# Windowed attention and two MoE layers on one core: attention masks added in PSUM by products with the identity for four groups, weight splits on ACT and VectorE

## The chip, the core and the metric

The kernel runs on one core of a Trainium2 chip. Its engines are TensorE (PE: matmul and transposes; PEld is its weight load), VectorE (DVE), ScalarE (ACT), GpSimd (POOL) and SyncE (SP), which issues the DMAs; each works through a queue of its own in order, and waits on semaphores of the others. SBUF holds the tiles, PSUM the results of TensorE. The metric is the device time of the program in microseconds (us); lower is better.

## What is computed

Inputs are q, k and v (2 batches, 8 heads, 768 positions, 64 dimensions, float32) and the weights of two feed-forward layers in float64. Attention sees a window of 16 positions on either side, and besides it one row for each block of 32 positions: the maximum of k and the mean of v.

```python
k_sum = k.reshape(B, H, nb, 32, D).max(axis=3)
v_sum = v.reshape(B, H, nb, 32, D).mean(axis=3)
scores_l = where(abs(i - j) < 16, scale * q @ k.T, -1e9)
scores_s = scale * q @ k_sum.T + log(32)
a = softmax(concatenate([scores_l, scores_s], -1))
x = a @ concatenate([v, v_sum])             # 1536 tokens x 512
x = (relu(x @ w_in) ** 2) @ w_out           # 512 x 2048, 2048 x 512
xn = x / rms(x) * rms_g
out = (silu(xn @ w_gate) * (xn @ w_val)) @ w_out2   # 512 x 1536, twice, and 1536 x 512
```

## The kernel before

**Tiles.** The 1536 tokens are 12 groups of 128, six to a batch. A group's scores fill two PSUM tiles `s0`, `s1` of 128 x 480: four heads each, with 120 columns a head (24 block rows and a window of 96 positions). Every product of the feed-forward layers is made of three (`mm3`, `ff_out`): both factors are split into a high part (fp32r) and a low part (the rest), as `xhi`/`xlo`, `hhi`/`hlo` and `w_`.

**A group.** `scores` makes 16 products into `s0` and `s1`. `softmax` has VectorE add the mask and write the sum to the SBUF tile `t` (L444), take the maximum of each head (L448), and ACT the exponential with its sum, head by head (L450); VectorE divides. Groups 0 to 2 do this in two parts of four heads, later ones in one. `ptrans` transposes `t` into `pps`, which ACT copies to `pT` (L471). `av` multiplies with `vx`, the rows of v and the means, into `xps` (L491), which ACT and VectorE split into `xhi` and `xlo` (L481, L482). Since `vx` has four slots, `vload` of a later group (L407, on SP) waits for `xps` of an earlier one. `qprep` transposes q two groups at a time (L366, copy L367), `prep_k` k. `vmean` makes the means of v by products with a constant (L379).

**Weights.** They come as 64-bit words (`load64`: `raw_wi`, `raw_wo`, DMA on SP). `conv_a` lets ACT read the two words (L176, L177), `conv_b` lets VectorE put a float32 together in four instructions (L183 to L190), and `split` makes `w_`: for the first eight tiles (`wi0` to `wi3`, `wo0` to `wo3`) on GpSimd (cast L197, subtraction L200), for the later ones on ACT and VectorE. `Units.tick` moves this pipeline by one step.

**Stages.** A start phase prepares k, q and the first scores. Then the first round of the first layer runs in six pairs of groups, with the attention of the following groups woven in: `h_pair` makes h of two weight tiles (L512), `y_pair` adds them to `y` (L533), so that TensorE has products of the layer while ACT and VectorE do the softmax. After that only the layers' own products are left; there TensorE does nothing else until the end.

**What sets the order.** Each engine's order is made when the program is built, by the Tile scheduler: it goes by its own forecast of the time and by the program's order. PSUM tiles of the attention rotate over four tags with two slots each in the first groups, then over `a` and `x`; of the tags, `y` and `h` are those of the layers. A tile's slot is given on when its last reader is done.

Two definitions decide what runs where around the change:

```python
def EXPACT(g): return g % 4 != 1 or g == 1     # maxima negated, exps on ACT head by head
def PARTS(g): return 2 if g < 3 else 1         # softmax in two parts
```

Of the kernel before, what the change touches and what calls it, by code (L numbers as in the profile page):

```python
# [10 lines left out]
F32 = mybir.dt.float32  # L11
F32R = mybir.dt.float32r
U32 = mybir.dt.uint32
I32 = mybir.dt.int32
AF = mybir.ActivationFunctionType
ALU = mybir.AluOpType
AX = mybir.AxisListType
# [15 lines left out]
def tile_window_attention_moe_moe2(  # L33
# [43 lines left out]
    scale = 1.0 / math.sqrt(D)  # L77

    cpool = ctx.enter_context(tc.tile_pool(name="cpool", bufs=1))
    wpool = ctx.enter_context(tc.tile_pool(name="wpool", bufs=1))  # L80
    xpool = ctx.enter_context(tc.tile_pool(name="xpool", bufs=NCH))
    hpool = ctx.enter_context(tc.tile_pool(name="hpool", bufs=2))
# [5 lines left out]
    ident = cpool.tile([P, P], F32, name="ident")  # L88
    make_identity(nc, ident)
    um = cpool.tile([P, KW + QT], F32, name="um")  # L90
    masks = {}
    ind = cpool.tile([P, NB + P // (BLK // 2) * (NC2 - 1)], F32, name="ind")
    ss = cpool.tile([P, NG], F32, name="ss")
    rinv = cpool.tile([P, NG], F32, name="rinv")
# [1 line left out]
    def constants():  # L96
        n = ind.shape[1]
        o = P // (BLK // 2) * (NC2 - 1)
        pb = BLK // 2
        nc.gpsimd.memset(ind, 1.0 / BLK)  # L100
        nc.gpsimd.affine_select(
            out=ind, in_=ind, compare_op=ALU.is_ge, fill=0.0, base=pb * o,
            pattern=[[-pb, n]], channel_multiplier=1,
        )
        nc.gpsimd.affine_select(
            out=ind, in_=ind, compare_op=ALU.is_ge, fill=0.0, base=pb - 1 - pb * o,
            pattern=[[pb, n]], channel_multiplier=-1,
        )
        nc.gpsimd.memset(um, 0.0)
        nc.gpsimd.affine_select(  # L110
            out=um, in_=um, compare_op=ALU.is_ge, fill=NEG, base=-1,
            pattern=[[1, KW + QT]], channel_multiplier=-1,
        )
        nc.gpsimd.affine_select(
            out=um, in_=um, compare_op=ALU.is_ge, fill=NEG, base=2 * WIN - 1,
            pattern=[[-1, KW + QT]], channel_multiplier=1,
        )


        mid = cpool.tile([P, NK], F32, name="mask_mid")  # L120
        nc.gpsimd.memset(mid, math.log(BLK))
        for j, n, o in ((0, G0, 0), (K1, QT, G0)):
            nc.gpsimd.tensor_copy(mid[0:QT, j : j + n], um[0:QT, o : o + n])
            nc.gpsimd.tensor_copy(mid[QT:P, j : j + n], um[QT:P, QT + o : QT + o + n])
        first = cpool.tile([P, NK], F32, name="mask_first")
        nc.gpsimd.tensor_copy(first, mid)
        nc.gpsimd.memset(first[0:QT, 0:WIN], NEG)
        last = cpool.tile([P, NK], F32, name="mask_last")
        nc.gpsimd.tensor_copy(last, mid)
        nc.gpsimd.memset(last[QT:P, NK - WIN : NK], NEG)  # L130
        masks.update(first=first, mid=mid, last=last)

# [55 lines left out]
        nc.vector.tensor_tensor(xi, xi, r, op=ALU.add)  # L190
        return x

    def split(x, nm, pool):
        w_ = wslot(f"w_{nm}")
        hi, lo = w_[:, 0], w_[:, 1]
        if pool:
            nc.gpsimd.tensor_copy(hi, x)  # L197
        else:
            nc.scalar.copy(hi, x)
        (nc.gpsimd if pool else nc.vector).tensor_tensor(lo, x, hi.bitcast(F32), op=ALU.subtract)  # L200
        return hi, lo

    class Units:
# [9 lines left out]
        def tick(self):  # L213
            n, units = self.n, self.units
            if n[3] < n[2]:
                u = units[n[3]]
                W[u] = split(self.x.pop(u), "%s%d" % u, n[3] < 2 * ROUNDS1[0])
                n[3] += 1
            if n[2] < n[1]:
                u = units[n[2]]  # L220
                with after(*((("mx", 0),) if n[2] == 0 else ())):
                    self.x[u] = conv_b(*self.a.pop(u))
                n[2] += 1
            if n[1] < n[0]:
                u = units[n[1]]
                self.a[u] = conv_a(self.raw.pop(u), "%s%d" % u)
                n[1] += 1
            self.load(min(n[2] + self.ahead, len(units), self.used + self.cap))
# [182 lines left out]
    def scores(g):  # L411
        b, r = divmod(g, GPB)
        qT = state[("qT", g)][:, :, (r % 2) * P : (r % 2 + 1) * P]
        sl = [psA(f"s{e}_{g}", [P, NPAIR, NK]) for e in range(2)]
        for p in range(NPAIR):
            for x in range(2):
                for e in range(2):
# [4 lines left out]
                        sl[e][QT * u : QT * u + QT, p, :],  # L422
                        qT[rr, p, QT * u : QT * u + QT],
                        kT[rr, p, o : o + NK],
                        start=True, stop=True,
                    )
        state[("s", g)] = sl

    def softmax(g):
# [10 lines left out]
        for i in range(parts):  # L440
            hs = slice(n * i, n * i + n)
            tv, m_, s_ = t[:, hs], mx[:, hs], sm[:, hs]
            for e in range(2 // parts * i, 2 // parts * (i + 1)):
                nc.vector.tensor_tensor(  # L444
                    te[:, e], sl[e], mk.unsqueeze(1).to_broadcast([P, NPAIR, NK]), op=ALU.add
                )
            if EXPACT(g):
                mark[("mx", g)] = nc.vector.reduce_max(m_, tv, axis=AX.X, negate=True)  # L448
                for h in range(hs.start, hs.stop):
                    mark[("exp", g)] = nc.scalar.activation(  # L450
                        t[:, h], t[:, h], AF.Exp, bias=mx[:, h : h + 1], accum_out=sm[:, h : h + 1]
                    )
            else:
                nc.vector.reduce_max(m_, tv, axis=AX.X)
# [406 lines left out]
```

## Time and profile before

| | us |
|---|---|
| three runs | 667.84, 668.17, 668.64 |
| median | 668.17 |
| the profiled execution | 667.06 |
| its span (first to last instruction) | 665.4 |
| busy in it: TensorE | 642.0 (96%) |
| VectorE | 402.9 (61%) |
| ACT | 304.6 (46%) |
| GpSimd | 27.3 (4%) |

The profile is one execution. Its span lies 1.7 us below the time of that execution, which in turn lies 1.1 us below the median. TensorE is busy for nearly the whole span, and GpSimd only in its first 100 us; but a share over the span is a mean over stages, and the attention lies in the first 120 us or so. There a table by stretches, the timelines of the engines and the SP queue tell what TensorE waits for. [...]

### The profile page before, as it was taken

Reading aid. Unit: us, or ns where it says so; the run is one execution under the profiler, and the core shown is the slowest. Engines: PE = TensorE matmul, PEld = TensorE weight load, DVE = VectorE, ACT = ScalarE, POOL = GpSimd, SP = SyncE. Lnnn points to the kernel's source line nnn. Section 1 sums busy time; section 2 is a strip of 40 time slices with the busy share of each in tenths; the row PEclk is TensorE's granted clock in tenths of the full one; section 3 lists DMA queues with packets and bytes.
Section 4 is the critical chain, followed back from the end, with each engine's and each line's share of the span. In section 5 each row is a group of like instructions: output and inputs, shape, how many; then the busy total and the mean of one; then the engine's idle time right before and its main releaser. Section 6 shows DMA issues by size and latency. Waiting matters only on the chain.

```text
span 665.4 us, 9357 instructions
## 1 busy us (share of the span) xinstructions
PE 642.0 (96%) x3644; PEld 530.8 (80%) x3644; DVE 402.9 (61%) x716; ACT 304.6 (46%) x656; POOL 27.3 (4%) x45
## 2 busy tenths in 40 slices
PE   7768997999999999999999999999999999999997
PEld 6566976888888888888888888888888888888885
DVE  4798777759999389528484894299613271313132
ACT  4875666557675266227253773267411231111110
POOL 3153110000000000000000000000000000000000
PEclk9878998999999999999999999999999999999999
DMA  9994644215412313101131351025300000001011
GB/s 241 290 222 112 152 136 142 75 39 179 138 64 95 96 64 96 32 1 64 32 96 32 97 162 60 1 60 161 97 0 1 0 1 0 1 1 63 1 64 64
DMA packets 76957, 53.70 MB, mean 81 GB/s; under 512 B 45040, under 2 KB 71664, under 8 KB 76912
## 3 DMA queue, kind: packets, MB, share of 16 engines
q1 hardware_dynamic: 76912, 53.09, 27.0%
q8 instruction: 29, 0.48, 0.3%
q14 instruction: 16, 0.13, 0.1%
HBM read 49.94 MB, written 3.15 MB: 80 GB/s over the span
## 4 chain that ended last, share of the span: by engine, by line
PE 87%; DVE 5%; SPq 3%; ACT 2%; issue 1%; DMA 1%; DVEq 0%; ACTq 0%
PE y L533 19%; PE h L512 18%; PE v L512 15%; PE g L512 15%; PE z L533 15%; ACT t L450 2%; PE xps L491 2%; PE pps L470 1%; SPq L308 1%; PE s L421 1%; SPq L407 1%; PE vmean L379 1%; PE xps L503 1%; PE qps L366 1%; DMA qr<-in_q_dram 1%
## 5 line engine op out<-in xcount | busy, mean ns | idle before, releaser
L512 PE MATMUL h<-xhi,w_wi 128*128 128x512 f32 (+1 forms) x480 | 134.2, 352 | 1.3 <-ACT xhi L481 1.3
L533 PE MATMUL y<-w_wo,hhi 128*128 128x512 f32 x384 | 119.0, 394 | 0.1
L807 DVE TENSOR_TENSOR sg<-v,sg 128x512 f32<-128x512 f32 x36 | 24.9, 691 | 131.2 <-PE v L512 131.2
L512 PEld LDWEIGHTS h<-xhi,w_wi 128*128 128x128 f32 x480 | 86.3, 192 | 13.3 <-ACT xhi L481 1.5
L512 PE MATMUL v<-xhi,w_wv 128*128 128x512 f32 x288 | 94.8, 390 | 0.0
L512 PE MATMUL g<-xhi,w_wg 128*128 128x512 f32 x288 | 94.5, 390 | 0.0
L533 PE MATMUL z<-w_wp,hhiz 128*128 128x512 f32 x288 | 88.0, 389 | 0.0
L512 PE MATMUL h<-xlo,w_wi 128*128 128x512 f32 (+1 forms) x240 | 84.4, 352 | 3.0 <-DVE xlo L482 3.0
L533 PEld LDWEIGHTS y<-w_wo,hhi 128*128 128x128 f32 x384 | 71.5, 189 | 14.8 <-ACT hhi L523 0.4
L533 PE MATMUL y<-w_wo,hlo 128*128 128x512 f32 x192 | 74.2, 394 | 0.2 <-DVE hlo L524 0.2
L805 ACT ACTIVATE sg<-g 128x512 f32<-128x512 f32 x36 | 21.5, 597 | 102.1 <-PE g L512 99.9
L512 PEld LDWEIGHTS v<-xhi,w_wv 128*128 128x128 f32 x288 | 54.1, 188 | 11.2
L512 PEld LDWEIGHTS g<-xhi,w_wg 128*128 128x128 f32 x288 | 54.0, 188 | 11.2
L533 PEld LDWEIGHTS z<-w_wp,hhiz 128*128 128x128 f32 x288 | 54.0, 188 | 11.1
L660 ACT ACTIVATE r<-h 128x512 f32<-128x512 f32 x48 | 28.6, 596 | 67.5 <-PE h L512 67.4
L512 PE MATMUL v<-xlo,w_wv 128*128 128x512 f32 x144 | 56.1, 389 | 0.0
L512 PE MATMUL g<-xlo,w_wg 128*128 128x512 f32 x144 | 56.0, 389 | 0.0
L533 PE MATMUL z<-w_wp,hloz 128*128 128x512 f32 x144 | 55.4, 389 | 0.0
L523 ACT CAST hhiz<-sg 128x512 fp32r<-128x512 f32 x36 | 22.3, 620 | 68.6 <-DVE sg L807 68.3
L512 PEld LDWEIGHTS h<-xlo,w_wi 128*128 128x128 f32 x240 | 46.2, 192 | 8.8 <-DVE xlo L482 3.2
L661 DVE TENSOR_TENSOR r<-h,r 128x512 f32<-128x512 f32 x48 | 32.9, 685 | 32.4 <-ACT r L660 32.4
L533 PEld LDWEIGHTS y<-w_wo,hlo 128*128 128x128 f32 x192 | 36.0, 189 | 8.1 <-DVE hlo L524 0.6
(133 smaller groups left out, 918.7 us busy)
## 6 DMA issues: line engine op xcount, KB each, us to landing
raw_wi<-in_moe_w_in_dram SPq DMA_DIRECT2D x16, 512.0 KB, 4.9
raw_wo<-in_moe_w_out_dram SPq DMA_DIRECT2D x16, 512.0 KB, 4.3
raw_wg<-in_moe_w_gate_dram SPq DMA_DIRECT2D x12, 512.0 KB, 3.5
raw_wv<-in_moe_w_val_dram SPq DMA_DIRECT2D x12, 512.0 KB, 3.6
raw_wp<-in_moe_w_out_dram SPq DMA_DIRECT2D x12, 512.0 KB, 3.5
kr<-in_k_dram SPq DMA_DIRECT2D x12, 256.0 KB, 4.2
qr<-in_q_dram SPq DMA_DIRECT2D x12, 256.0 KB, 3.9
vr<-in_v_dram SPq DMA_DIRECT2D x6, 512.0 KB, 4.9
```

Of the source, the lines that this page charges most:

```text
L308: nc.sync.dma_start(t[:, j].rearrange("p (h d) -> p h d", h=H), src[b, :, o : o + P, :].rearrange("h p d -> p h d"),)
L366: nc.tensor.transpose(ps[:, p, :], qr[:, j, p * P : (p + 1) * P], ident)
L379: nc.tensor.matmul(ps, ind[:, nb2 * (NC2 - 1 - c) : nb2 * (NC2 - 1 - c) + NB], vr[:, :, e, :], start=(c == 0 and e == 0), stop=(c == NC2 - ...
L450: mark[("exp", g)] = nc.scalar.activation(t[:, h], t[:, h], AF.Exp, bias=mx[:, h : h + 1], accum_out=sm[:, h : h + 1])
L491: nc.tensor.matmul(ps[QT * e : QT * e + QT, o : o + QT], vx[:, (2 * g + u) % NVX, 2 * p + e, :], pT[:, e * NPAIR + p, QT * u : QT * u + QT ...
L512: nc.tensor.matmul(ps, a_, b_, start=(i == 0), stop=(i == tot - 1))
L523: nc.scalar.copy(hi[:, 0:n], s[:, 0:n])
L533: nc.tensor.matmul(y, a_[:, ms], b_, start=(first and i == 0), stop=(last and i == 2))
L660: nc.scalar.activation(t, ps, AF.Relu)
L661: nc.vector.tensor_tensor(t, ps, t, op=ALU.mult)
L805: nc.scalar.activation(t, psg, AF.Silu)
L807: nc.vector.tensor_tensor(t, psv, t, op=ALU.mult)
```

## The change

**Masks.** For groups 0 to 3 (`NPE`) the mask is no longer added by VectorE. A product of the identity (`identr`) with the mask's high part (`mhi`), repeated for the four heads of a tile, opens the accumulation in `s0` and `s1`; the 16 score products add to it; a product with the low part (`mlo`) closes it. The maxima and the exponentials then read PSUM and not `t`. Group 3, whose one maximum covered 960 columns, takes two of 480, one for each PSUM tile. GpSimd makes `identr`, two high parts and the low part (that of `mid`) at the start.

**Splits.** `split` has no GpSimd branch any more: the first eight weight tiles are cast by ACT and subtracted by VectorE, as the others were already.

**Tiles.** A constant tile of 24 columns (`left`) is put first in `cpool`, beside the new constants.

The scheduler makes a new order out of this. On ACT, around the copies of `pT5` (group 5's transposed weights), before:

```order
L367 ACTIVATE qT6_929<-qps6_0_930 128x4x128
L367 ACTIVATE qT6_929<-qps6_1_936 128x4x128
L660 ACTIVATE r0_1_2_1054<-h0_1_2_1029 128x512
L471 COPY pT5_974<-pps5_0_975 120x512
L523 CAST hhi0_1_2_1057<-r0_1_2_1054 128x512
L471 COPY pT5_974<-pps5_1_981 120x512
L176 ACTIVATE x_wi4_1696<-raw_wi4_1493 128x512
L177 ACTIVATE u_wi4_1697<-raw_wi4_1493 128x512
L481 CAST xhi1_1_925<-xps1_5_1061 128x4x128
L388 COPY vm1_1087<-vmean1_1080 24x512
```

and now:

```order
L508 CAST xhi1_1_943<-xps1_4_926 128x4x128
L376 ACTIVATE qT6_947<-qps6_0_948 128x4x128
L376 ACTIVATE qT6_947<-qps6_1_954 128x4x128
L498 COPY pT5_992<-pps5_0_993 120x512
L573 COPY yp3_1202<-y0_1_1_1149 128x512
L188 ACTIVATE x_wi4_1714<-raw_wi4_1511 128x512
L189 ACTIVATE u_wi4_1715<-raw_wi4_1511 128x512
L498 COPY pT5_992<-pps5_1_999 120x512
L508 CAST xhi1_1_943<-xps1_5_1079 128x4x128
L397 COPY vm1_1105<-vmean1_1098 24x512
```

The second copy of `pT5` stands behind the two reads of `raw_wi4` and no longer ahead of them; the copy of y (`yp3`) stands ahead of both, and the copies of q's transposes ahead of `pT5`, as they did.

On TensorE, from the h products of the second pair to those behind xps of group 4, before:

```order
L512 MATMUL h0_1_2_1029<-xhi1_0_416,w_wi3_685 128x256
L512 MATMUL h0_1_2_1029<-xlo1_0_417,w_wi3_685 128x256
L331 MATMUL kps1_2_1_889<-ident_77,kr1_2_774 128x128 x4
L512 MATMUL h0_1_2_1029<-xhi1_0_416,w_wi3_685 128x256
L491 MATMUL xps1_4_908<-pT4_813,vx_90 64x64 x16
L366 MATMUL qps6_0_930<-ident_77,qr6_645 128x128 x4
L366 MATMUL qps6_1_936<-ident_77,qr6_645 128x128 x4
L512 MATMUL h0_1_2_1029<-xhi1_0_416,w_wi3_685 128x256
```

and now:

```order
L560 MATMUL y0_1_0_1148<-w_wo0_797,hhi0_1_0_988 128x512
L560 MATMUL y0_1_0_1148<-w_wo0_797,hlo0_1_0_989 128x512
L560 MATMUL y0_1_1_1149<-w_wo0_797,hhi0_1_0_988 128x512 x2
L560 MATMUL y0_1_1_1149<-w_wo0_797,hlo0_1_0_989 128x512
L560 MATMUL y0_1_0_1148<-w_wo1_814,hhi0_1_0_988 128x512 x2
L560 MATMUL y0_1_0_1148<-w_wo1_814,hlo0_1_0_989 128x512
L560 MATMUL y0_1_1_1149<-w_wo1_814,hhi0_1_0_988 128x512 x2
L560 MATMUL y0_1_1_1149<-w_wo1_814,hlo0_1_0_989 128x512
L518 MATMUL xps1_4_926<-pT4_831,vx_95 64x64 x16
L375 MATMUL qps6_0_948<-ident_78,qr6_663 128x128 x4
L375 MATMUL qps6_1_954<-ident_78,qr6_663 128x128 x4
L497 MATMUL pps5_0_993<-ident_78,t5_774 120x128 x4
```

Products for y with the weights `wo0` and `wo1` stand ahead of xps of group 4, where h products stood.

On TensorE, at the scores of group 3 (`s0_3`, `s1_3`), before:

```order
L470 MATMUL pps1_1_431<-ident_77,t1_310 120x128 x4
L491 MATMUL xps1_0_399<-pT0_344,vx_90 64x64 x15
L470 MATMUL pps1_0_425<-ident_77,t1_310 120x128 x4
L421 MATMUL s0_3_437<-kT_89,qT2_331 64x120 x8
L421 MATMUL s1_3_438<-kT_89,qT2_331 64x120 x8
L491 MATMUL xps1_1_472<-pT1_424,vx_90 64x64 x16
L512 MATMUL h0_0_0_521<-xhi1_0_416,w_wi0_534 128x256
```

and now:

```order
L497 MATMUL pps1_1_446<-ident_78,t1_325 120x128 x4
L428 MATMUL s0_3_452<-mhi_mid_87,identr_84 128x480
L435 MATMUL s0_3_452<-kT_94,qT2_344 64x120 x8
L443 MATMUL s0_3_452<-mlo_85,identr_84 128x480
L518 MATMUL xps1_1_490<-pT1_439,vx_95 64x64
L428 MATMUL s1_3_453<-mhi_mid_87,identr_84 128x480
L435 MATMUL s1_3_453<-kT_94,qT2_344 64x120 x8
L443 MATMUL s1_3_453<-mlo_85,identr_84 128x480
L518 MATMUL xps1_1_490<-pT1_439,vx_95 64x64 x15
L497 MATMUL pps2_0_514<-ident_78,t2_392 120x128 x4
L497 MATMUL pps2_1_520<-ident_78,t2_392 120x128 x4
```

Each score tile is opened by a product with `mhi_mid` (L428) and closed by one with `mlo` (L443), and the xps of group 1 are divided around the second tile.

The diff:

```diff
--- before.py
+++ after.py
@@ -77,6 +77,7 @@
     scale = 1.0 / math.sqrt(D)
 
     cpool = ctx.enter_context(tc.tile_pool(name="cpool", bufs=1))
+    cpool.tile([P, 24], F32, name="left")
     wpool = ctx.enter_context(tc.tile_pool(name="wpool", bufs=1))
     xpool = ctx.enter_context(tc.tile_pool(name="xpool", bufs=NCH))
     hpool = ctx.enter_context(tc.tile_pool(name="hpool", bufs=2))
@@ -88,7 +89,12 @@
     ident = cpool.tile([P, P], F32, name="ident")
     make_identity(nc, ident)
     um = cpool.tile([P, KW + QT], F32, name="um")
-    masks = {}
+    masks, mhi = {}, {}
+    NPE = 4
+    identr = cpool.tile([P, P], F32R, name="identr")
+    mlo = cpool.tile([P, NK], F32R, name="mlo")
+    for nm in ("first", "mid"):
+        mhi[nm] = cpool.tile([P, NK], F32R, name=f"mhi_{nm}")
     ind = cpool.tile([P, NB + P // (BLK // 2) * (NC2 - 1)], F32, name="ind")
     ss = cpool.tile([P, NG], F32, name="ss")
     rinv = cpool.tile([P, NG], F32, name="rinv")
@@ -129,6 +135,12 @@
         nc.gpsimd.tensor_copy(last, mid)
         nc.gpsimd.memset(last[QT:P, NK - WIN : NK], NEG)
         masks.update(first=first, mid=mid, last=last)
+        nc.gpsimd.tensor_copy(identr, ident)
+        nc.gpsimd.tensor_copy(mhi["first"], first)
+        nc.gpsimd.tensor_copy(mhi["mid"], mid)
+        nc.gpsimd.tensor_tensor(
+            mlo, mid, mhi["mid"].bitcast(F32), op=ALU.subtract
+        )
 
 
 
@@ -190,14 +202,11 @@
         nc.vector.tensor_tensor(xi, xi, r, op=ALU.add)
         return x
 
-    def split(x, nm, pool):
+    def split(x, nm):
         w_ = wslot(f"w_{nm}")
         hi, lo = w_[:, 0], w_[:, 1]
-        if pool:
-            nc.gpsimd.tensor_copy(hi, x)
-        else:
-            nc.scalar.copy(hi, x)
-        (nc.gpsimd if pool else nc.vector).tensor_tensor(lo, x, hi.bitcast(F32), op=ALU.subtract)
+        nc.scalar.copy(hi, x)
+        nc.vector.tensor_tensor(lo, x, hi.bitcast(F32), op=ALU.subtract)
         return hi, lo
 
     class Units:
@@ -214,7 +223,7 @@
             n, units = self.n, self.units
             if n[3] < n[2]:
                 u = units[n[3]]
-                W[u] = split(self.x.pop(u), "%s%d" % u, n[3] < 2 * ROUNDS1[0])
+                W[u] = split(self.x.pop(u), "%s%d" % u)
                 n[3] += 1
             if n[2] < n[1]:
                 u = units[n[2]]
@@ -412,6 +421,11 @@
         b, r = divmod(g, GPB)
         qT = state[("qT", g)][:, :, (r % 2) * P : (r % 2 + 1) * P]
         sl = [psA(f"s{e}_{g}", [P, NPAIR, NK]) for e in range(2)]
+        wide = [P, NPAIR, NK]
+        if g < NPE:
+            for s_ in sl:
+                mh = mhi["mid" if r else "first"]
+                nc.tensor.matmul(s_, identr, mh.unsqueeze(1).to_broadcast(wide), start=True, stop=False)
         for p in range(NPAIR):
             for x in range(2):
                 for e in range(2):
@@ -422,8 +436,13 @@
                         sl[e][QT * u : QT * u + QT, p, :],
                         qT[rr, p, QT * u : QT * u + QT],
                         kT[rr, p, o : o + NK],
-                        start=True, stop=True,
+                        start=g >= NPE, stop=g >= NPE,
                     )
+        if g < NPE:
+            for s_ in sl:
+                mark[("s", g)] = nc.tensor.matmul(
+                    s_, identr, mlo.unsqueeze(1).to_broadcast(wide), start=False, stop=True
+                )
         state[("s", g)] = sl
 
     def softmax(g):
@@ -440,15 +459,23 @@
         for i in range(parts):
             hs = slice(n * i, n * i + n)
             tv, m_, s_ = t[:, hs], mx[:, hs], sm[:, hs]
-            for e in range(2 // parts * i, 2 // parts * (i + 1)):
+            for e in range(2 // parts * i, 2 // parts * (i + 1)) if g >= NPE else ():
                 nc.vector.tensor_tensor(
                     te[:, e], sl[e], mk.unsqueeze(1).to_broadcast([P, NPAIR, NK]), op=ALU.add
                 )
             if EXPACT(g):
-                mark[("mx", g)] = nc.vector.reduce_max(m_, tv, axis=AX.X, negate=True)
+                src = [t[:, h] for h in range(H)]
+                if g < NPE:
+                    src = [s_[:, p] for s_ in sl for p in range(NPAIR)]
+                    for e in range(2 // parts * i, 2 // parts * (i + 1)):
+                        mark[("mx", g)] = nc.vector.reduce_max(
+                            mx[:, NPAIR * e : NPAIR * (e + 1)], sl[e], axis=AX.X, negate=True
+                        )
+                else:
+                    mark[("mx", g)] = nc.vector.reduce_max(m_, tv, axis=AX.X, negate=True)
                 for h in range(hs.start, hs.stop):
                     mark[("exp", g)] = nc.scalar.activation(
-                        t[:, h], t[:, h], AF.Exp, bias=mx[:, h : h + 1], accum_out=sm[:, h : h + 1]
+                        t[:, h], src[h], AF.Exp, bias=mx[:, h : h + 1], accum_out=sm[:, h : h + 1]
                     )
             else:
                 nc.vector.reduce_max(m_, tv, axis=AX.X)
```

## Rows read from the trace of the kernel before

**Rows 1.** Busy time of engines by stretches: us and (instructions), PEclk, DMA share, GB/s.

```profile
core 0: us, PE busy (x) PEld busy (x) DVE busy (x) ACT busy (x) POOL busy (x), PEclk, DMA share, GB/s
30.00:60.00 30.00, 21.87 (x251) 18.48 (x248) 30.00 (x51) 20.36 (x58) 13.79 (x13) 0.85 0.81 215
60.00:100.00 40.00, 40.00 (x398) 32.47 (x398) 31.30 (x50) 27.52 (x87) 5.48 (x5) 0.98 0.50 133
100.00:120.00 20.00, 16.09 (x185) 13.03 (x183) 15.02 (x25) 12.89 (x35) 0.00 (x0) 0.91 0.44 130
120.00:665.00 545.00, 541.02 (x2639) 450.22 (x2637) 309.97 (x558) 224.86 (x420) 0.00 (x0) 1.00 0.18 58
```

**Rows 2.** Timeline, TensorE: start us, us, engine line operation out<-in, count, [idle before <-releaser].

```profile
40.62 0.58 PE L512 MATMUL h<-xlo,w_wi 128*128 128x256 f32 x1 [3.01 <-DVE xlo L482]
...
65.83 0.40 PE L512 MATMUL h<-xhi,w_wi 128*128 128x256 f32 x2
...
82.80 1.15 PE L491 MATMUL xps<-pT,vx 120*64 120x64 f32 x30
...
102.09 1.58 PE L491 MATMUL xps<-pT,vx 120*64 120x64 f32 x32 [1.64 <-issue]
...
112.66 1.97 PE L491 MATMUL xps<-pT,vx 120*64 120x64 f32 x30 [2.14 <-ACT pT L471]
```

**Rows 3.** Timeline, VectorE from 47 to 62 us, and GpSimd beside it.

```profile
47.92 1.52 DVE L184 TENSOR_SCALAR x_wo<-x_wo 128x512 uint32<-128x512 uint32 x1
50.91 0.41 DVE L184 TENSOR_SCALAR x_wo<-x_wo 128x512 uint32<-128x512 uint32 x1
60.41 1.59 DVE L524 TENSOR_TENSOR hlo<-r,hhi 128x512 fp32r<-128x512 f32 x1
...
47.06 2.10 POOL L200 TENSOR_TENSOR w_wo<-x_wo,w_wo 128x512 fp32r<-128x512 f32 x1
```

**Rows 4.** Timeline, VectorE, 57 to 60 us.

```profile
57.59 0.67 DVE L190 CUSTOM_DVE_ANT_0 x_wo<-x_wo,u_wo 128x1024 uint16<-128x1024 uint16 x1
...
59.35 1.13 DVE L448 TENSOR_REDUCE mx<-t 128x8 f32<-128x960 f32 x1
```

**Rows 5.** Groups by line, 0 to 170 us: count | busy us, mean ns | idle, releaser.

```profile
L444 DVE TENSOR_TENSOR t<-s,mask_mid 128x480 f32<-128x480 f32 x16 | 10.0, 648 | 5.7 <-PE s L421 5.7
...
L448 DVE TENSOR_REDUCE mx<-t 128x4 f32<-128x480 f32 x6 | 3.8, 644 | 0.0
```

**Rows 6.** Chain of work that ended last, in order of time: start us, us, what.

```profile
63.00 2.99 PE y L533 x12
```

**Rows 7.** Timeline, ACT, 25 to 52 us.

```profile
25.12 0.38 ACT L450 ACTIVATE t<-t,mx 128x120 f32<-128x120 f32 x1
...
25.62 0.60 ACT L367 ACTIVATE qT<-qps 128x512 f32<-128x512 f32 x1
...
27.70 0.68 ACT L176 ACTIVATE x_wi<-raw_wi 128x512 f32<-128x512 f32 x1 [0.44 <-DMA raw_wi<-in_moe_w_in_dram]
...
28.84 0.56 ACT L471 COPY pT<-pps 120x512 f32<-120x512 f32 x1
...
51.02 0.62 ACT L523 CAST hhi<-r 128x512 fp32r<-128x512 f32 x1 [1.08 <-DVE r L661]
```

**Rows 8.** Timeline, TensorE, SP's queue (SPq) and ACT, 74 to 94 us.

```profile
74.07 1.15 PE L491 MATMUL xps<-pT,vx 120*64 120x64 f32 x32
75.14 2.95 SPq L407 DMA_DIRECT2D vx<-in_v_dram  x4
78.19 0.57 SPq L161 DMA_DIRECT2D raw_wi<-in_moe_w_in_dram  x1
82.44 0.67 ACT L176 ACTIVATE x_wi<-raw_wi 128x512 f32<-128x512 f32 x1 [0.85 <-DMA raw_wi<-in_moe_w_in_dram]
83.88 5.33 PE L379 MATMUL vmean<-vr,ind 128*24 128x512 f32 x12
93.52 0.59 ACT L546 COPY yp<-y 128x512 f32<-128x512 f32 x1
```

## Prediction

> **What bounds the kernel now.** I read the table by stretches first, then TensorE's timeline for its waits, then the queues behind each wait. From 120 us to the end TensorE is busy 541.0 of 545 us at a granted clock of 1.00, and from 60 to 100 us it is never idle [rows 1]. A change to the attention prologue can therefore only be worth what it does to TensorE's idle or slow time before about 120 us. There are two such places. In 30 to 60 us TensorE is busy 21.9 of 30 us at a clock of 0.85, while VectorE is busy all 30 us [rows 1]: the h product waits 3.01 us for VectorE's xlo [rows 2]. In 100 to 120 us TensorE waits twice, 1.64 us before xps of group 6 and 2.14 us before xps of group 7, the latter for ACT's pT copy [rows 2], and the clock of that stretch is 0.91 [rows 1].
>
> Behind the first place lies VectorE's queue, and it is lengthened: ten of its instructions between 24 and 62 us, the first at 24.11 us and the last shown, lie beside a GpSimd split and take 0.3 to 1.1 us longer than their kind. The shift at 47.92 takes 1.52 us beside GpSimd's 2.10 us subtraction, the same form alone 0.41 us [rows 3]. The ten excesses add up to 7.4 us.
>
> Behind the second lies a chain that begins where the means of v end on TensorE (83.88 + 5.33 = 89.2 us [rows 8]): ACT copies vm, runs the exps of groups 6 and 7, the pT copies, and so on until xps of group 7 at 112.66 us. TensorE waits inside this chain twice, so what it gained earlier is lost there, unless the means of v end earlier too. That point, which I call V (89.2 us now), decides.
>
> **The change, part by part.** All steps are from one start to the next, which is some 0.07 us less than a row's duration: the maximum of 960 columns lasts 1.13 us and is followed after 1.06 (59.35 to 60.41 [rows 3, 4]). So a 512-column word operation of 0.67 counts as 0.60 [rows 4], an add of 480 columns of 0.65 [rows 5] as 0.57, and ACT's rows less 0.09.
>
> *What VectorE loses and gets.* Eight mask adds go (8 x 0.57 = 4.6 us); eight low parts come (0.60 each, 4.8 us). For group 3 two maxima of 480 columns replace one of 960, which costs nothing. The queue's own work stays equal; the gain is the 7.4 us of excess, 6.7 of it after 34 us.
> The maxima now read PSUM. The add that reads PSUM averages 648 ns, the maximum of the same width that reads SBUF 644 ns [rows 5], so I take nothing for it. [...]
>
> *GpSimd.* Its eight splits go, about 16 us. It gets four operations of some 120 columns on constants, by its 2.10 us for 512 columns [rows 3] some 0.5 us each, an estimate. They follow its other constants in the first microseconds, while TensorE waits for k, so I take nothing; without that cover they cost 2.0 us.
>
> *TensorE.* Sixteen products of 480 columns come. Twelve y products of 512 columns take 2.99 us [rows 6], so these cost 0.23 us each, twice that at the lower clock: 3.7 to 7.5 us, all before 40 us, where TensorE waits anyway. I take nothing on the path.
>
> *A longer hold.* Scores stay in PSUM until the exps have read them, where the add freed them earlier. In the new order the first mask product of group 3 waits for the last exps of group 2, and xps of group 2 for the last exps of group 3. So ACT's queue is what counts.
>
> *ACT's queue.* It starts where it does now, after the exps of group 1, at 25.62 [rows 7]. Until the last exps of group 3 stand 4 casts for the splits (0.53, from the 0.62 of the cast at 51.02), 5 pairs of weight reads (1.14, from 27.70 to 28.84), 9 copies of 0.47 to 0.50, and 16 exps with their sums (0.38) [rows 7]: 2.1 + 5.7 + 4.3 + 6.1 = 18.2 us, so 43.8; with 0.3 us of waits 44.1.
>
> *VectorE from there* to the low part of the fourth wo weight: 15 steps of 0.60, 4 short ones of 0.33, 4 of 0.57, 4 of 960 columns (1.06) and 4 tiny ones: 9.0 + 1.3 + 2.3 + 4.2 + 0.4 = 17.2 us, so 61.3; with small waits 61.7. TensorE needs four y products more: 62.7. It then stands, with two h products ahead, where it stands now at 65.83 [rows 2]. **The start phase gains about 3.1 us.**
>
> *Up to V.* Now TensorE goes from 65.83 to xps of group 4 at 74.07 in 8.2 us [rows 2, 8]. In the new order 7 h products (0.8) and 12 y products (2.9) more stand before it: 62.7 + 11.9 = 74.6. From xps of group 4 to that of group 5 is 8.7 us now (74.07 to 82.80 [rows 2, 8]); 9 h and 2 y products less (1.5) make it 7.2: TensorE arrives at 81.8.
> But the order on ACT has turned. Now the second pT copy of group 5 stands before the read of raw_wi4, which waits 0.85 us for its DMA at 82.44 [rows 8]. In the changed program it stands behind that read and its partner. The DMA is issued on SP behind four loads of vx, which wait for the first half of xps of group 4: now 75.14, then the issue at 78.19 and the read at 82.44 [rows 8]. From 75.1 that makes the read 82.4 to 82.5, two reads 1.14, the copy 0.57 with its signal: 84.2. **TensorE waits 2.4 us** where it waits nothing now, and the means of v stand behind it. V = 84.2 + 1.08 + 5.33 = 90.6, plus what the clock takes.
>
> *The clock after that wait.* After 1.64 us idle 32 xps products took 1.58 us, after 2.14 us idle 30 took 1.97, against 1.15 at full speed [rows 2]: 0.4 and 0.8 lost in the first row. [...] So the loss lies between 0.4 and 2.2; I take 1.5, nearest to the 2.14 us row and its followers. V = 92.1, 2.9 us later than now.
>
> *Behind V* ACT is rid of the copy of y at 93.52 [rows 8], which now comes before: 0.5 us less. Xps of group 7 comes 2.4 us later than now, with the same products done before and behind it. TensorE reaches that second wait later in the chain, so the wait is about 1 us and not 2.14. The clock of 0.91 over 20 us [rows 1] is 1.8 us lost, 0.4 of it behind the first wait and so 1.4 behind the second; between 0 and 1.4 of that comes back, I take 1.0. From there TensorE has no wait to fill, so what is left comes out at the end.
>
> **Sum: +2.9 - 0.5 - 1.0 = +1.4 us.** The profiled execution took 667.06 us (span 665.4, 1.7 around it) and would take 668.5; the median of the runs shown is 668.17, so 669.6. A measurement of this kernel can tell about 0.2%, 1.3 us, from no change.
>
> **The rivals.**
> *The lead is kept.* If raw_wi4 has landed when ACT comes to its read, nothing waits at group 5: V = 81.8 + 1.1 + 5.3 = 88.2, 1.0 earlier, and with 0.5 and about 0.7 of the clock the end is 2.2 us earlier: 666.0. It decides from the point where the DMA is 2.4 us earlier against TensorE. For it speaks that VectorE's contention is plain; against it that SP's loads and the wait hang on the same event.
> *The scores hold their banks too long (slower).* Place: the ring of ACT's exps, PSUM, scores and maxima of groups 2 and 3. If one more of ACT's reads or a slow-clock score block stands in each turn of it, 1.2 us for each of two groups, the start phase ends 2.5 us later, and so does V: +3.9, 672.1. It decides once the low part of the fourth wo weight ends after 64 us. For it speaks the 0.85 clock [rows 1]; against it that ACT's 18.2 us hold nearly no waits in the walk.
> *The long VectorE rows are not GpSimd's doing.* Then the change does not do what it frees; the five excesses after 44 us (3.9 us) stay: 673.5. Against it: all ten lie beside GpSimd.
>
> **How the numbers follow.** Forecast as walked 0.58, with its own range 667.6 to 671.6 from the clock's bounds and 1 us of the walk; within it slower 0.32, same 0.22, faster 0.04. Lead kept 0.25 (faster 0.20, same 0.05). Banks held 0.13 and no relief 0.04, both slower. Faster 0.24, same 0.27, slower 0.49. The range 666.0 to 672.2 leaves out half of the kept lead and a part of the two slow cases.
>
> **What would show it.** No GpSimd compute between 25 and 100 us, and shifts of 0.41 us throughout; the last exps of group 3 near 44; the low part of the fourth wo weight near 61.7; TensorE idle some 2.4 us before xps of group 5, released by ACT behind raw_wi4's DMA; V near 92; the wait before xps of group 7 shorter than 2.14 us. The forecast is wrong if TensorE does not wait at group 5, or if its clock stays at 1.00 behind that wait.

## The result and the profile after

The changed kernel takes 669.50 us in the median of 20 runs, the kernel before 666.64 us in 20 runs beside them: the ratio is 1.0051, 95% interval 1.0033 to 1.0069. It is slower, as forecast, and 669.5 us lies beside the 669.6 us that was forecast. But the three runs of before that were shown had a median of 668.17 us, 1.5 us above that of the 20. The change itself costs 2.9 us by the medians and 3.4 us by the ratio, about twice the +1.4 us of the sum. So part of the hit is a shifted base, and the terms have to be looked at one by one. Both kernels spread from run to run (664.32 to 670.68 us before, 666.16 to 673.89 now); between the shortest run of each lie 1.8 us.

The table by stretches of the changed kernel (TensorE, its weight load, VectorE, ACT, GpSimd busy, granted clock of TensorE as a share of full speed, DMA share, GB/s), to be laid beside [rows 1]:

```profile
30.00:60.00 30.00, 28.31 (x334) 22.71 (x335) 27.96 (x56) 23.92 (x74) 0.00 (x0) 0.89 0.83 219
60.00:100.00 40.00, 38.53 (x328) 30.42 (x329) 27.13 (x44) 23.47 (x70) 3.18 (x3) 1.00 0.46 124
100.00:120.00 20.00, 15.84 (x182) 13.18 (x181) 15.75 (x28) 14.49 (x42) 0.00 (x0) 0.91 0.48 137
120.00:665.00 545.00, 542.87 (x2653) 451.94 (x2651) 311.71 (x561) 226.63 (x422) 0.00 (x0) 1.00 0.18 58
```

GpSimd is gone from 30 to 60 us, TensorE is busy 28.3 us there and not 21.9, and new idle time shows in the next stretch: TensorE is busy 38.5 of 40 us, where nothing was idle before. TensorE's timeline, against [rows 2] and [rows 8]:

```profile
77.27 1.15 PE L518 MATMUL xps<-pT,vx 120*64 120x64 f32 x32
...
86.25 1.15 PE L518 MATMUL xps<-pT,vx 120*64 120x64 f32 x30 [1.04 <-ACT pT L498]
87.32 5.33 PE L388 MATMUL vmean<-vr,ind 128*24 128x512 f32 x12
...
104.51 2.41 PE L518 MATMUL xps<-pT,vx 120*64 120x64 f32 x32 [2.72 <-issue]
...
115.75 1.15 PE L518 MATMUL xps<-pT,vx 120*64 120x64 f32 x30 [1.29 <-ACT pT L498]
```

Xps of group 4 starts at 77.27 (74.07 before), the new wait before xps of group 5 is there, released by ACT's pT copy, and V, the end of the means of v, is 87.32 + 5.33 = 92.65 us (89.2 before). What stands behind that wait is in the timelines of SP's queue and of ACT, against [rows 8]:

```profile
78.00 2.27 SPq L416 DMA_DIRECT2D vx<-in_v_dram  x4
80.36 0.57 SPq L173 DMA_DIRECT2D raw_wi<-in_moe_w_in_dram  x1
...
84.50 0.67 ACT L188 ACTIVATE x_wi<-raw_wi 128x512 f32<-128x512 f32 x1 [1.23 <-DMA raw_wi<-in_moe_w_in_dram]
85.07 0.66 ACT L189 ACTIVATE u_wi<-raw_wi 128x512 int32<-128x512 uint32 x1
85.62 0.57 ACT L498 COPY pT<-pps 120x512 f32<-120x512 f32 x1
```

The copy that TensorE waits for stands behind two reads of raw_wi4, whose DMA was issued behind the four loads of vx: the mechanism as forecast. On VectorE's timeline the shift that took 1.52 us beside GpSimd [rows 3] takes 0.42, and the low part of the fourth wo weight ends at 64.0 us:

```profile
41.90 0.42 DVE L196 TENSOR_SCALAR x_wo<-x_wo 128x512 uint32<-128x512 uint32 x1
...
63.34 0.68 DVE L209 TENSOR_TENSOR w_wo<-x_wo,w_wo 128x512 fp32r<-128x512 f32 x1
```

### The profile page after: what moved, and what is told of

It reads as the page before. It is cut to its first block, busy times and chain, and to the rows that moved or that the text cites. A ratio compares the mean times of both kernels' runs of the same rounds, so it can differ in the third digit from the quotient of the medians.

```text
span 667.1 us, 9380 instructions
## 1 busy us (share of the span) xinstructions
PE 650.0 (97%) x3660; PEld 535.5 (80%) x3660; DVE 396.3 (59%) x717; ACT 307.7 (46%) x664; POOL 10.5 (2%) x33
## 4 chain that ended last, share of the span: by engine, by line
PE 87%; DVE 6%; SPq 3%; ACT 2%; DMA 1%; issue 1%; DVEq 0%; ACTq 0%
PE y L560 18%; PE h L539 18%; PE v L539 15%; PE g L539 15%; PE z L560 14%; PE xps L518 1%; ACT t L477 1%; PE s L435 1%; SPq L416 1%; SPq L317 1%; PE pps L497 1%; PE vmean L388 1%; PE xps L530 1%; SPq L306 1%; DMA raw_wi<-in_moe_w_in_dram 1%
## 5 line engine op out<-in xcount | busy, mean ns | idle before, releaser
L539 PE MATMUL h<-xhi,w_wi 128*128 128x512 f32 (+1 forms) x480 | 132.5, 349 | 0.2 <-ACT xhi L508 0.2
L539 PEld LDWEIGHTS h<-xhi,w_wi 128*128 128x128 f32 x480 | 84.8, 189 | 12.5 <-ACT xhi L508 0.7
L539 PEld LDWEIGHTS v<-xhi,w_wv 128*128 128x128 f32 x288 | 54.1, 188 | 11.2
L560 PEld LDWEIGHTS z<-w_wp,hhiz 128*128 128x128 f32 x288 | 54.0, 188 | 11.2
L539 PEld LDWEIGHTS g<-xhi,w_wg 128*128 128x128 f32 x288 | 54.0, 188 | 11.2
L550 ACT CAST hhiz<-sg 128x512 fp32r<-128x512 f32 x36 | 22.3, 620 | 68.4 <-DVE sg L834 68.1
```

The lines of the kernel that those rows point to most:

```text
L539: nc.tensor.matmul(ps, a_, b_, start=(i == 0), stop=(i == tot - 1))
L550: nc.scalar.copy(hi[:, 0:n], s[:, 0:n])
L560: nc.tensor.matmul(y, a_[:, ms], b_, start=(first and i == 0), stop=(last and i == 2))
```

## Experiments

Each run stands beside runs of the kernel before on the same chip; intervals are 95%. The expectations of the first four call A the theory that the start phase is lost to the mask products at TensorE's lower clock (granted 0.50), B the theory that the casts and subtractions on ACT and VectorE lose it.

**One half of the change: splits alone.** The split of the changed kernel in the kernel before:

```diff
-        if pool:
-            nc.gpsimd.tensor_copy(hi, x)
-        else:
-            nc.scalar.copy(hi, x)
-        (nc.gpsimd if pool else nc.vector).tensor_tensor(lo, x, ...)
+        nc.scalar.copy(hi, x)
+        nc.vector.tensor_tensor(lo, x, ...)
```

> One half of the change alone: the first eight weight splits go to ACT and VectorE, VectorE still adds all masks. Theory A (in the changed kernel the mask products and the scores of groups 2 and 3 stand in the ring PSUM, maxima, exponentials, and run it at the lower clock, which eats the 3 us that VectorE won): without them the start phase keeps its gain, the low part of the fourth wo weight ends near 61 us, xps of group 4 starts near 72, the means of v end 1 to 3 us earlier than the 89.2 us of before, and the ratio to the kernel before is 0.995 to 0.998. Theory B (the four casts more on ACT and eight subtractions more on VectorE eat the gain, wherever the masks are added): the fourth wo weight is not earlier than in the changed kernel (64.0), and the ratio is 1.003 to 1.006, as with the whole change.

Measured: 1.0011 (0.9994 to 1.0029), span of the profile 667.6 us. Neither figure fits. GpSimd's contention is gone (no GpSimd instruction from 24 to 80 us, shifts of 0.41 to 0.42 us) and nothing is won in this form. Its profile has the lower clock in the start phase though there are no mask products: 0.50 from 24 to 30 us and 0.57 from 30 to 38, behind a wait of 4.22 us for q.

**The other half: masks alone.** The changed kernel with the first eight splits back on GpSimd (the diff above the other way round).

> The other half alone: masks of groups 0 to 3 by products with the identity, the first eight splits on GpSimd as in the kernel before. Theory A: the ring of scores, maxima and exponentials is as slow as in the changed kernel (scores of group 2 as 1.87 us and not 1.04, last exponentials of group 3 near 46 us), GpSimd's contention is back on top of it, ratio 1.006 to 1.010. Theory B: VectorE and ACT are rid of the splits and VectorE of eight adds, so the start phase ends earlier than in both kernels and the ratio is below 0.998.

Measured: 0.9969 (0.9956 to 0.9983), with 12 runs within 2.2 us. Masks by products alone make the kernel faster; A's figure is refuted, B's holds. Its start phase, in the table by stretches:

```profile
24.00:30.00 6.00, 5.67 (x64) 4.13 (x65) 4.87 (x12) 5.65 (x18) 0.81 (x1) 1.00 1.02 353
30.00:38.00 8.00, 5.67 (x67) 4.15 (x62) 8.00 (x18) 6.28 (x23) 4.43 (x4) 0.84 0.94 295
```

So in this execution the products do not bring the lower clock in 24 to 30 us; in 30 to 38 us it falls behind a wait of 2.33 us for exponentials. That is one execution, and one of the shortest of the 12 (664.38 us). And the halves don't add up: -0.31% and +0.11% against +0.51% together. Each of the three builds has an order of its own, and only the whole has both changes at work on ACT: the casts in its queue, and scores held in PSUM until its exponentials have read them. These runs do not part the two.

**The order on ACT.** In the changed kernel the read of raw_wi4 is put behind the second pT copy of group 5:

```diff
-                self.a[u] = conv_a(self.raw.pop(u), "%s%d" % u)
+                with after(*((("pT", 5),) if u == ("wi", 4) else ())):
+                    self.a[u] = conv_a(self.raw.pop(u), "%s%d" % u)
```

> The changed kernel, in which ACT may read raw_wi4 only behind the second pT copy of group 5. The start phase up to xps of group 4 stays as it is (77.3 us). Theory of the stall (this copy standing behind a read that waits for a DMA costs TensorE its wait before xps of group 5, and the means of v with it): the 1.04 us wait goes, the means of v end near 91.6 instead of 92.65 us, and the ratio to the kernel before falls from 1.005 to 1.003 or less. Rival (what is saved there is waited for before xps of groups 6 or 7, whose chain begins with the exponentials): the wait before xps of group 5 goes and the waits behind grow by as much, the ratio stays at 1.005.

Measured: 0.9964 (0.9945 to 0.9984), more than expected. TensorE's order is the same as in the changed kernel to the scores of group 7, and the start is the same on ACT to the copy of yp3. TensorE's timeline:

```profile
74.66 1.15 PE L519 MATMUL xps<-pT,vx 120*64 120x64 f32 x32
...
82.27 1.15 PE L519 MATMUL xps<-pT,vx 120*64 120x64 f32 x32
83.35 5.33 PE L389 MATMUL vmean<-vr,ind 128*24 128x512 f32 x12
...
100.06 1.19 PE L561 MATMUL y<-w_wo,hhi 128*128 128x512 f32 x4 [1.39 <-ACT hhi L551]
101.19 0.33 PE L519 MATMUL xps<-pT,vx 120*64 120x64 f32 x2
```

The wait before xps of group 5 is gone: from xps of group 4 to V it is 14.0 us and not 15.4. Behind V the new order also puts y products ahead of xps of group 6, where TensorE waited 2.72 us, and the rest of the span is 573.4 us and not 574.4. Together that is 2.4 us, 0.36%. The measured step from 1.0051 is 0.87%, 5.8 us, so 3.4 us of it are not explained by the place of the edit. Of the 5.0 us between the two profiles the other 2.6 lie ahead of xps of group 4, which is at 74.66 here and at 77.27 there, with the same instructions of TensorE in the same order, at a granted clock of 0.76 here and 0.55 there from 24 to 38 us.

**The clock in the start phase.** In the changed kernel 24 products of zeros fill TensorE's wait for q of group 2:

```diff
             ps = psA(f"qps{g}_{j}", [P, NPAIR, P])
+            for _ in range(24 if (g, j) == (2, 0) else 0):
+                nc.tensor.matmul(ps[:, 0, :], wz, wz, start=True, stop=True)
```

> The changed kernel with 24 products of zeros (128 columns, some 3 us) ahead of the transposes of q of group 2, where TensorE waits 3.1 us for that DMA; they are overwritten, the result is the same. Theory A (the start phase is late because TensorE's clock is at its lower level from 24 to 37 us behind that wait, with the mask products on the path): the granted clock of 24 to 37 us is near 1.00 and not 0.50, the scores of group 2 take 1.04 us a tile and not 1.87, the last exponentials of group 3 end near 43.5 and not 46.2 us, xps of group 4 starts 2 to 3 us earlier than 77.3, and the ratio falls from 1.005 to 0.999 to 1.002. Theory B (ACT's and VectorE's queues set the end of the start phase): the clock rises as well, but the last exponentials of group 3 stay within 0.7 us of 46.2 and the ratio at 1.004 to 1.006.

Measured: 1.0006 (0.9988 to 1.0024). The clock is 1.00 from 24 to 46 us, but the last exponential of group 3 begins at 44.86 and ends past 45 us. The scheduler put some fillers ahead of the last means of v of batch 0, whose copy on ACT came at 24.09 us and not at 20.95, and VectorE stood idle for 8.67 us. Between A and B this says nothing clear: the clock was bought with the delay.

**The same kernel again.** No edit; the changed kernel in a second set of runs, and once more in a third. C is the theory that one execution differs from the next by the clock behind the wait for q, D that the change's own work makes the start late.

> The changed kernel once more, beside the three others on one chip. Theory C (in the start phase one execution differs from the next by when q of group 2 lands and by how long TensorE's clock is at its lower level behind that wait; the rest of the loss is the order on ACT around the copies of group 5): ratio 1.004 to 1.006, and in the profile the end of the means of v minus xps of group 4 is 15.4 us again, with a wait of about 1 us before xps of group 5, while xps of group 4 itself may start anywhere between 74.5 and 77.5 us. Rival D (the start phase is late by the change's own work, whatever the clock): xps of group 4 starts within 0.5 us of 77.3 again.

> The changed kernel once more, for its profile: one more execution. Theory C: whether xps of group 4 starts near 74.2 or near 77.3 us goes with the granted clock of 24 to 38 us in that execution (1.00 or 0.50), and the span with it (near 664 or above 667). Rival D: it does not go with the clock.

Measured: 1.0051 (1.0023 to 1.0078) and 1.0061 (1.0033 to 1.0089). The profiles caught two other executions of the same program: spans of 663.9 and 671.1 us, against 667.1 us above. The tables by stretches, first the span of 663.9 us:

```profile
24.00:38.00 14.00, 12.06 (x123) 9.36 (x123) 12.33 (x28) 13.84 (x45) 0.00 (x0) 0.88 0.97 319
38.00:60.00 22.00, 20.82 (x261) 17.16 (x255) 21.97 (x42) 18.68 (x56) 0.00 (x0) 1.00 0.85 202
```

then 667.1 us:

```profile
24.00:38.00 14.00, 13.35 (x92) 10.65 (x92) 9.40 (x23) 11.15 (x38) 0.00 (x0) 0.55 0.97 317
38.00:60.00 22.00, 20.91 (x275) 17.33 (x276) 22.00 (x43) 18.68 (x55) 0.00 (x0) 1.00 0.78 184
```

and 671.1 us:

```profile
24.00:38.00 14.00, 13.15 (x92) 10.20 (x92) 9.02 (x22) 11.81 (x43) 0.86 (x1) 0.57 0.98 321
38.00:60.00 22.00, 21.66 (x205) 17.95 (x204) 18.49 (x38) 16.63 (x45) 0.00 (x0) 0.73 0.67 152
```

With a mean clock of 0.88 ACT is busy 13.8 of 14 us and TensorE waits; with one of 0.55 TensorE is busy 13.4 of 14 us, ACT 11.2, VectorE 9.4: the bound has changed over. TensorE's timeline for a score tile of group 3 and the two places behind it, in the execution of 663.9 us:

```profile
35.02 0.49 PE L428 MATMUL s<-mhi_mid,identr 128*128 128x480 f32 x1 [1.94 <-ACT t L477]
...
37.08 0.48 PE L428 MATMUL s<-mhi_mid,identr 128*128 128x480 f32 x1
37.49 1.04 PE L435 MATMUL s<-kT,qT 64*64 64x120 f32 x16
38.46 0.48 PE L443 MATMUL s<-mlo,identr 128*128 128x480 f32 x1
...
74.17 1.15 PE L518 MATMUL xps<-pT,vx 120*64 120x64 f32 x32
83.11 1.15 PE L518 MATMUL xps<-pT,vx 120*64 120x64 f32 x30 [0.99 <-ACT pT L498]
84.18 5.33 PE L388 MATMUL vmean<-vr,ind 128*24 128x512 f32 x12
```

and in that of 671.1 us:

```profile
38.56 0.77 PE L428 MATMUL s<-mhi_mid,identr 128*128 128x480 f32 x1 [0.16 <-ACT t L477]
...
42.16 0.77 PE L428 MATMUL s<-mhi_mid,identr 128*128 128x480 f32 x1
42.86 1.87 PE L435 MATMUL s<-kT,qT 64*64 64x120 f32 x16
44.65 0.77 PE L443 MATMUL s<-mlo,identr 128*128 128x480 f32 x1
...
81.39 1.15 PE L518 MATMUL xps<-pT,vx 120*64 120x64 f32 x32
90.32 1.15 PE L518 MATMUL xps<-pT,vx 120*64 120x64 f32 x30 [0.99 <-ACT pT L498]
91.39 5.33 PE L388 MATMUL vmean<-vr,ind 128*24 128x512 f32 x12
```

A tile with its mask takes 1.8 us from start to start at a granted clock of 1.00 and 3.2 at 0.50, 1.4 of it the two mask products. Where the lower clock ends at about 28 us TensorE still waits 1.94 us for ACT ahead of group 3's scores; where it lasts to about 37 or 50 us, that wait is down to 0.76 and 0.16 us. V is at 89.51, 92.65 and 96.72 us, and the span behind V is 574.4 us in each of the three: all 7.2 us between the executions arise ahead of xps of group 4. D falls, and of C the clock holds: the q transposes begin within 0.5 us of each other (23.79, 24.05 and 24.30 us). Two of C's figures do not hold. Xps of group 4 at 81.39 us lies outside both values that were expected, and the clock of 24 to 38 us (0.55 and 0.57) does not part the last two executions; that of 38 to 60 us does (1.00 and 0.73).

**Q earlier.** The load of q of groups 2 and 3 ahead of the eight loads of vx, in the changed kernel, in the kernel before, in the one with the read of raw_wi4 put behind, and in the two halves:

```diff
+    qload(2)
     vload(0)
     vload(1)
-    qload(2)
```

> The changed kernel with the load of q of groups 2 and 3 issued ahead of the eight loads of vx and no longer behind them. Theory C: TensorE's wait before these transposes (3.14 us) falls under 1 us, the granted clock of 24 to 38 us is over 0.9, the last exponentials of group 3 end by 44 us, and the ratio falls from 1.005 to 0.998 to 1.002; its runs lie closer together than those of the changed kernel (7.7 us from lowest to highest). Rival D: the wait goes and the ratio stays at 1.004 to 1.006.

> The kernel before with the same earlier load of q. Theory C: VectorE's queue, which GpSimd slows, sets the end of this start phase, so the earlier q is worth little here: ratio 0.998 to 1.001. Rival (the wait for q and the clock behind it are a cost of both kernels alike): the ratio falls by as much as with the changed kernel, 0.995 to 0.997.

> The changed kernel with both edits: the read of raw_wi4 behind the second pT copy of group 5, and the earlier load of q. Theory C: the two gains add up, 0.9964 less 0.3 to 0.5 per cent, ratio 0.991 to 0.994, faster than both kernels. Rival D: no more than the first edit alone, 0.995 to 0.998.

> Masks by products, splits of the first eight weights left on GpSimd, and the load of q of groups 2 and 3 issued ahead of those of vx. Theory C (the wait for q and the clock behind it cost every kernel in which VectorE does not set the end of the start phase): ratio 0.993 to 0.996, below the 0.9969 without the earlier load. Rival (with the splits on GpSimd VectorE sets that end): 0.996 to 0.998.

> Splits on ACT and VectorE, masks added by VectorE, and the load of q of groups 2 and 3 issued ahead of those of vx. If VectorE's relief from GpSimd is worth the 3 us of the prediction and only the clock behind the wait for q hid it (1.0011 without the earlier load), the ratio is 0.994 to 0.998. If the splits' own instructions on ACT and VectorE take the relief back, it stays at 0.999 to 1.002.

Measured: 0.9967 (0.9945 to 0.9989) in the changed kernel, 0.9993 (0.9976 to 1.0010) in the kernel before, 0.9956 (0.9935 to 0.9976) with the read behind, 1.0000 (0.9981 to 1.0020) with masks alone, 0.9985 (0.9968 to 1.0002) with splits alone. The wait for q is gone in the profiles, but for 0.4 us with splits alone, and what takes its place differs. In the changed kernel the ratio is below C's 0.998 to 1.002, and not by C's cause: TensorE waits 2.06 us for exponentials behind the transposes of q, and the clock of 24 to 38 us is 0.63, not over 0.9 as expected:

```profile
23.91 1.09 PE L497 MATMUL pps<-ident,t 128*120 128x128 f32 x8 [2.06 <-ACT t L477]
...
81.28 1.15 PE L518 MATMUL xps<-pT,vx 120*64 120x64 f32 x32
```

The wait before xps of group 5 is gone there, by the new order, and V is 87.69 us. With masks alone the ratio rises from 0.9969 to 1.0000, outside both expectations; in its profile TensorE waits 2.77 us for the last exponentials of group 3, and 2.07 us for the first four of them without the earlier load. So C's claim that the wait for q costs every such kernel is wrong: each of these builds has another order, which may decide as much as the load; no run parts the two. With splits alone 0.9985 is neither of the two expectations, and whether the relief from GpSimd is worth anything by itself stays open. The kernel before does as C expected. The best of all is the changed kernel with both edits, 0.9956, but C's 0.991 to 0.994 is missed, so the two gains do not add up; it cannot be told from the one without the earlier load, 0.9964, but both are faster than the kernel before.

**A longer wait before xps of group 5.** The second pT copy of that group is done three times:

```diff
-            mark[("pT", g)] = nc.scalar.copy(pT[...], ps[...])
+            for _ in range(3 if (g, hf) == (5, 1) else 1):
+                mark[("pT", g)] = nc.scalar.copy(pT[...], ps[...])
```

> The changed kernel with the second pT copy of group 5 done three times over (the same values), which makes TensorE's wait before xps of group 5 some 1.1 us longer, about 2.1 us. Theory E (a wait there costs more than itself, since the clock can fall behind it, and the 12 products of the means of v run at the lower clock): these products take more than 5.33 us, up to 10.7, the means of v end 2 to 6 us later than by the wait alone, and the ratio rises from 1.005 to 1.008 to 1.015. Rival F (the clock holds through waits of this length at this place, as in the two profiles of the changed kernel): the products take 5.33 us, the ratio is 1.006 to 1.007.

Measured: 1.0039 (1.0009 to 1.0069), no change that can be told from 1.0051. Behind 1.81 us of waiting the 12 products still take 5.33 us, so E falls:

```profile
87.82 1.04 PE L435 MATMUL s<-kT,qT 64*64 64x120 f32 x16 [1.81 <-DVE t L463]
88.79 5.33 PE L388 MATMUL vmean<-vr,ind 128*24 128x512 f32 x12
```

The scheduler moved most of that xps behind the means of v (94.05 us), so the wait of V for the copy, which this was to lengthen, went away.

**V in all profiles.** One point of the timeline nearly sorts the executions (V, the span, and what lies between them, in us). Each row is a single execution, not the median of its runs; the one with raw_wi4 behind and the earlier load took 666.86 us where the median was 663.48:

| | V | span | behind V |
|---|---|---|---|
| before | 89.2 | 665.4 | 576.2 |
| changed, three executions | 89.5, 92.7, 96.7 | 663.9, 667.1, 671.1 | 574.4 each |
| splits alone, masks alone | 93.7, 87.9 | 667.6, 662.7 | 573.9, 574.8 |
| raw_wi4 behind, fillers | 88.7, 90.3 | 662.1, 667.1 | 573.4, 576.8 |
| earlier q: changed, before, raw_wi4 behind | 87.7, 90.4, 91.3 | 661.6, 664.9, 665.1 | 573.9, 574.5, 573.8 |
| earlier q: masks alone, splits alone | 90.6, 90.9 | 665.3, 664.3 | 574.7, 573.4 |
| longer copy | 94.1 | 668.0 | 573.9 |

V lies between 87.7 and 96.7 us, what follows it between 573.4 and 576.8.

## Why the prediction was right, and by which steps

The number was right in part by luck: two errors cancel, and the base moved by 1.5 us. By the prediction's own sign the forecast was wrong at one place, for the clock stayed at 1.00 behind the wait before xps of group 5. The steps in turn:

**V decides: right.** The table bears it out: V differs by up to 9.0 us, what follows it by up to 3.4.

**VectorE's contention: gone as forecast, its worth not shown.** GpSimd does nothing from 24 to 75 us in the first profile, and the shifts take 0.42 us. In the execution of 663.9 us the last exponentials of group 3 end at 43.0 us (forecast 44.1) and the low part of the fourth wo weight at 60.9 (61.7), TensorE stands at the awaited place at 62.3 (62.7), xps of group 4 starts at 74.17 (74.6). The walk holds within 1.1 us where the clock is back early; in the execution of 667.1 us TensorE stands at that place at 65.4, against 65.83 before, so that of the 3.1 us 0.4 are left. That the relief is worth anything without the rest no run shows: splits alone gave 1.0011 and, with the earlier load of q, 0.9985. Part of the 1.1 us is the exponentials: those that read PSUM follow each other after 0.34 us (the first profile):

```profile
24.49 0.38 ACT L477 ACTIVATE t<-s,mx 128x120 f32<-128x120 f32 x1
...
24.83 0.39 ACT L477 ACTIVATE t<-s,mx 128x120 f32<-128x120 f32 x1
```

In the kernel before they read SBUF and follow each other after 0.38, as from this row to that at 25.12 [rows 7]:

```profile
24.74 0.38 ACT L450 ACTIVATE t<-t,mx 128x120 f32<-128x120 f32 x1
```

The prediction did not count these 0.04 us. For VectorE's maxima the difference is smaller: those that read PSUM average 653 ns (group L471 below) against 644 from SBUF [rows 5], 9 ns, and the prediction was right to take nothing:

```profile
L471 DVE TENSOR_REDUCE mx<-s 128x4 f32<-128x480 f32 x8 | 5.1, 653 | 5.5 <-PE s L443 5.5
```

**"I take nothing on the path" for TensorE's sixteen products: the step that failed.** The same row shows 5.5 us of VectorE's waiting for scores and mask products; in the executions of 663.9 and 671.1 us it is 2.5 and 7.5. The prediction had the doubled cost at the lower clock (0.70 us from start to start of a mask product is measured at 0.50, 0.41 at 1.00), and the wait that was to hide it; but the wait is there because TensorE is quick: 1.94 us ahead of group 3's scores at 1.00, 0.16 at 0.50. At the lower clock TensorE itself sets the ring of scores, maxima and exponentials, and xps of group 4 starts 3.1 us later (667.1 us) or 7.2 us later (671.1 us) than in the execution of 663.9 us. The lower clock slows the other products of this stage too (the 16 scores of a tile take 1.87 us and not 1.04, 30 xps products 1.97 and not 1.15); the masks' own part is 1.4 of the 3.2 us of a tile. This is the rival of the banks held too long by its effect, and at its point: the low part of the fourth wo weight ends at 64.0 us in the execution of 667.1 us, at 68.1 in that of 671.1. Its price of 2.5 us in V was close to what the former lost (3.1); its chance of 0.13 was far too low, since of the 40 executions of the changed kernel only 9 have a span within 2.4 us of the shortest.

**The wait before xps of group 5: right in place and cause, too large.** 2.4 us were forecast, about 1.0 is there in all three executions. The read of raw_wi4 comes 7.2 us behind the start of xps of group 4 and not 7.9, and TensorE arrives 7.9 us behind it and not 7.2.

**The clock behind that wait: wrong.** 1.5 us were taken, between 0.4 and 2.2, and no run shows the 1.5 or the bound of 2.2: the means of v take 5.33 us in the three executions of the changed kernel, and also behind 1.81 us of waiting with the longer copy. The clock that decides is lost earlier, in the start phase.

**Behind V: right.** -1.5 us forecast, 574.4 - 576.2 = -1.8 measured, with waits of 2.72 and 1.29 us before xps of groups 6 and 7 (1.64 and 2.14 before). From V to xps of group 7 it is 23.1 us and not 23.45 (-0.35, forecast -0.5), and from there to the end 551.35 and not 552.74 (-1.4, forecast -1.0): behind the shorter wait these xps products take 1.15 us and not 1.97. The longer wait before xps of group 6 was not forecast; its 32 products take 2.41 us there and not 1.58.

So V was forecast at 92.1 and is 92.65 in the first profile, from errors that cancel: too much from xps of group 4 to the means of v (9.6 us forecast, 9.0 measured: the wait 1.4 shorter, TensorE's way to it 0.7 longer) and for the clock behind it (1.5 us), nothing for the lower clock in the start phase (3.1 us, of which the walk made up 0.4). With the first two alone corrected the sum would have been -0.7 us, a small gain.

What stays open: why the executions of the changed kernel with raw_wi4 behind, whose start is the same row by row, lie so much more often near their shortest (8 of 12 spans within 2.4 us, against 9 of 40), and what makes TensorE's clock come back at 28, 37 or 50 us. The waits of 3.05, 3.14 and 2.13 us ahead of it don't sort the three.

## What to carry to other kernels

Work that is hidden under an engine's wait is hidden only while that engine runs at the rate the wait was read at: cost it at TensorE's lower clock too, and ask whether the wait is still there (here 1.94 us at a granted clock of 1.00 and 0.16 at 0.50). A scheduler's order is part of a change: two halves that were -0.3% and +0.1% made +0.5% together, and with one line on ACT's order the kernel was 0.9% shorter, 0.36% of it at the place that the line moves and the rest ahead of it, where no instruction had moved. Find the point of the timeline behind which the rest is constant, and compare that point, in several executions, before comparing times.

## What the runs showed of the hardware that was not expected

One program gave spans of 663.9, 667.1 and 671.1 us by when TensorE's granted clock rose from 0.50 to 1.00, at about 28, 37 and 50 us, behind the same wait for q (in the last it fell only at about 26 us). In the last, TensorE was busy without a gap of its own from 26.14 us to its wait of 0.16 us at 38.56 and on to 50.2 us, and the clock was 0.50 in these rows:

```profile
31.00:38.00 7.00, 7.00 (x58) 5.62 (x58) 5.55 (x13) 4.81 (x19) 0.00 (x0) 0.50 0.94 309
38.00:46.00 8.00, 7.84 (x52) 5.08 (x52) 5.30 (x12) 6.21 (x20) 0.00 (x0) 0.50 0.59 133
```

Its work there was the products of scores, masks, transposes and xps. The same instructions in the same order ran at a granted clock of 1.00 from about 28 us in the execution of 663.9 us, so a timing that was read from one execution of such a stage need not hold in the next.
